# One core, DeltaNet and a cosine feed-forward: 66 places of a hand-written order and the queue of seven transfers are changed

## The chip, the cores and the metric

The kernel runs on one core of one Trainium2 chip. The metric is the device time of one execution in microseconds (us). PE is the matrix engine, PEld its weight loads, DVE the vector engine, ACT the scalar engine, POOL the third elementwise engine (GpSimd), and SP an engine that here only begins DMA transfers. SP and ACT each have a DMA queue (SPq, ACTq); the profile lists what an engine begins there beside its own work.

## The reference, cut to what matters

```python
def _attn_ref(q, k, v, beta):            # 4 batches, 8 heads, 768 steps, 48 wide
    k_n = k / (np.linalg.norm(k, axis=-1, keepdims=True) + 1e-06)
    state = np.zeros((B, H, D, D))
    for t in range(S):
        kt, vt, bt = k_n[:, :, t], v[:, :, t], beta[:, :, t, None]
        y[:, :, t] = np.einsum('bhd,bhde->bhe', q[:, :, t], state)
        v_old = np.einsum('bhde,bhd->bhe', state, kt)
        state = state + bt[:, :, :, None] * np.einsum('bhd,bhe->bhde', kt, vt - v_old)
    return y

def _moe_ref(x, w_in, w_out):            # 3072 tokens x 384, inner width 2048
    h = x @ w_in
    g = h * np.cos(h)
    return g @ w_out
```

The attention's output y, with heads side by side, is the x of the feed-forward part.

## The kernel before, in words

**Units and pairs.** The 768 steps are cut into 24 units of 32 steps. For each unit n, for all 32 pairs of batch and head, the kernel

- loads k, q and v (`load`, L383, issue L398; from unit 6 on k and q also in the layout of `load_blocks`, L411, issue L417),
- turns k and q over (`turn`, L637, `turn_out`, L648, ACT copy L652), takes the norms of k (`norms_square` L557 on ACT, `norms_sum` L562 on DVE, `norms_root` L574 on POOL, `scale`, L603 to L611, on DVE),
- forms the products of keys and queries with keys (`gram`, PE L675; `gram_keys` and `gram_queries` read them on DVE),
- needs the inverse of a triangular 32 x 32 matrix. For units 0 and 1 this is done by matrix products on PE, a chain of doublings: `double` (PE L759), `double_copy` (ACT L767), `double_turn` (DVE L772 and L775), `double_add` (DVE L779). In the task names, double (n, level, half). From unit 2 on it is done on POOL, for two units (a pair m) at once: `gram_put` (L833) writes the matrices to device memory, `gram_get` (L854) reads them back one matrix to a partition, `invert` (POOL L879 and L886, in pieces inv (m, i)) does the substitution, `put` (L891) writes the inverse and `get` (L902 for units 2 and 3, L910 later) brings it home for unit n. Units 2 and 3 are inverted in halves and have the steps solve_half (PE L960), half_out (ACT L972), between (PE L960) and between_out (DVE L980) more,
- multiplies the carried state with keys and queries (`state`, PE L930), solves for the update (`solve`, PE L996 for units 2 and 3, L1002 else; solve_out, DVE L1014), updates the state (`update`, PE L1027; update_out, DVE), multiplies within the unit (`within`, PE L1045 for the first units, L1057; within_out, ACT L1070) and gives the features of the feed-forward part (`features`, PE L1078; features_out, ACT L1086).

**The feed-forward part.** Two units make a pair p of 256 tokens. For pair 0 the inner product is plain: `hidden` (p, f) (PE L1099), then the cosine gate as `hidden_turns` (ACT L1136), `hidden_rest` (DVE L1143), `hidden_cos` (ACT L1152), `hidden_gate` (DVE L1155). Later pairs use fewer products on sums of blocks: `x_sum` (L1188, on POOL or DVE), `layer` (p, i) (PE L1273), layer_out (ACT L1285, L1287, or DVE L1290), then the gate, `product` (PE L1355; tasks named out), `collect` (L1407) and `store` (L1422).

**The weights** arrive in 28 pieces: `narrow_load` (issue L518; tasks named weights), `narrow_split` on ACT (L528, L532), `narrow_shift` on DVE (L536) and `narrow_add` on POOL (L540; tasks named split, shift, add). `keep_warm` (PE L495, tasks named warm) are matmuls whose result nobody reads.

**The order.** Every such step is a task with a key such as ('gram_put', 2). `Order.run` emits 2199 tasks in the order of `Order.LINE`, a list of the tasks' numbers. All instructions of one engine are pinned to that order, and all DMA issues of SP and ACT are also pinned to one common order. So the list fixes each engine's program, and an engine that waits for one task holds all that is behind it. A task that begins DMAs is issued by SP, or by ACT when its key stands in the set `Order.OTHER`; for `x_sum`, `left`, `right` and a few more the same set picks POOL or DVE:

```python
    def queue(*key):
        return nc.scalar if key in Order.OTHER else nc.sync

    def either(key, one, two):
        return two if key in Order.OTHER else one
```

An issue on ACT stands in ACT's program between its copies and activations.

Of the kernel before, what the change touches and what calls it, by code (L numbers as in the profile page):

```python
# [59 lines left out]
class Order:  # L60

    OTHER = {
        ('v', 0), ('v', 1), ('gram_put', 2), ('gram_put', 3), ('inv', 1, 0), ('put', 1),
        ('gram_put', 4), ('v', 5), ('gram_get', 2), ('put', 2), ('gram_put', 6), ('v', 8),
        ('v', 9), ('blocks', 9, 0), ('blocks', 9, 1), ('put', 4), ('get', 10), ('v', 11),
        ('blocks', 11, 0), ('blocks', 11, 1), ('gram_put', 11), ('gram_get', 5), ('v', 12),
        ('gram_put', 13), ('gram_get', 6), ('get', 13), ('v', 14), ('blocks', 14, 0), ('v', 15),
        ('blocks', 15, 0), ('blocks', 15, 1), ('v', 16), ('gram_put', 16), ('v', 17), ('k', 18),
        ('v', 18), ('get', 18), ('v', 20), ('gram_put', 21), ('gram_get', 11), ('store', 0, 1),
        ('right', 4, 4), ('left', 1, 1, 0), ('left', 1, 3, 0), ('left', 1, 3, 1),  # L70
# [23 lines left out]
        ('left', 10, 3, 1), ('store', 10, 1), ('x_sum', 11, 'd'), ('x_sum', 11, 'e'),  # L94
        ('x_sum', 11, 'k'), ('x_sum', 11, 'g'), ('x_sum', 11, 'f'), ('left', 11, 1, 0),
        ('left', 11, 2, 0), ('left', 11, 1, 1), ('left', 11, 3, 0), ('left', 11, 3, 1),
        ('store', 11, 1), ('store_right', 11), ('weights', 2), ('weights', 3), ('weights', 4),
        ('weights', 9), ('weights', 11), ('weights', 12), ('weights', 13), ('weights', 14),
        ('weights', 15), ('weights', 17), ('weights', 23), ('weights', 24)
    }  # L100

    WARM_FIRST, WARMS = 5, 17
    LINE = """
# [1845 lines left out]
```

## Time and profile before

| what | number |
|---|---|
| time, median of 3 runs | 640.1 us (638.85 to 642.2) |
| the profiled execution's own time | 642.77 us |
| its span in the trace | 641.0 us (1.77 us lie around it) |
| granted PE clock, mean | 0.98 |
| PE busy | 612.1 us (95%) |
| DVE busy | 504.4 us (79%) |
| POOL busy | 435.1 us (68%) |
| ACT busy | 297.5 us (46%) |
| DMA | 50.75 MB in 215844 packets, 207384 of them under 512 B |

The times of engines are shares of the span, so the share that PE leaves idle is an upper bound for what a new order of the same work can win, apart from the clock: the granted clock is the speed that PE was given, 1.00 being full. All times in the text are us from the span's start. "Idle before, with a releaser" is the time that an engine stood before an instruction, and what ended it by the profile.

### The profile page before, as it was taken

To read this page: it belongs to the slowest core of one execution; us is meant where nothing else is said; L and a number is where in the kernel's file an instruction comes from. 1 tells how busy PE (TensorE), PEld (TensorE's weight loads), DVE (VectorE), ACT (ScalarE), POOL (GpSimd) and SP (SyncE) were. 2 spreads that over 40 slices of the span, in tenths; PEclk is the share of its full clock that TensorE was granted. 3 is DMA by queue.
4 is the path that set the end of the run, shared out by engine and by line. 5 is a ranking of instruction groups with operands and counts; after the bars stand their busy time and mean duration, and the time that the engine had idled before them with its cause. 6 is when DMAs were issued, how large, how long until landed. Compare 5 with 4: busy or idle time off the path is not lost.

```text
span 641.0 us, 24058 instructions
## 1 busy us (share of the span) xinstructions
PE 612.1 (95%) x10096; PEld 571.4 (89%) x10096; DVE 504.4 (79%) x1051; ACT 297.5 (46%) x533; POOL 435.1 (68%) x791
## 2 busy tenths in 40 slices
PE   6978788999999999999999999999999999999997
PEld 4857777788799998999999999999999999999997
DVE  5876736999999897788878788978878676757872
ACT  3546535645543543543743553643544443635440
POOL 4428877788888888786886786888884881212231
PEclk8897979999999999999999999999999999999999
DMA  9876656655354645446234445333225011000001
GB/s 187 218 169 174 136 130 134 148 87 83 72 87 74 103 74 96 69 67 111 42 52 87 75 79 91 54 45 70 45 35 101 18 31 23 20 3 15 13 20 30
DMA packets 215844, 50.75 MB, mean 79 GB/s; under 512 B 207384, under 2 KB 210744, under 8 KB 215736
## 3 DMA queue, kind: packets, MB, share of 16 engines
q1 hardware_dynamic: 161132, 32.34, 27.8%
q10 hardware_dynamic: 54300, 16.33, 12.1%
q8 instruction: 79, 1.29, 0.8%
q0 software_dynamic: 304, 0.54, 0.4%
q14 instruction: 29, 0.24, 0.1%
HBM read 38.95 MB, written 10.22 MB: 77 GB/s over the span
## 4 chain that ended last, share of the span: by engine, by line
PE 76%; DMA 8%; POOL 5%; DVE 5%; issue 2%; SPq 2%; ACT 1%; ACTq 1%; DVEq 0%; POOLq 0%
PE p_out L1355 30%; PE p_h L1273 28%; PE p_kq L930 3%; PE p_s L1027 3%; POOL part L879 2%; POOL z L886 2%; PE p_u L1002 2%; PE p_kq L1057 2%; PE p_g L675 2%; PE p_h L1099 2%; DMA qp<-in_q_dram 2%; PE p_h L1355 2%; DMA kp<-in_k_dram 2%; PE p_z L1078 1%; DMA w_sum<-z_dr 1%
## 5 line engine op out<-in xcount | busy, mean ns | idle before, releaser
L879 POOL TENSOR_TENSOR part<-z,gb 128x126 f32<-128x126 f32 (+23 forms) x321 | 141.6, 441 | 44.1 <-DMA gb<-g_dr 17.5
L886 POOL TENSOR_TENSOR z<-z,part 128x126 f32<-128x126 f32 (+23 forms) x321 | 142.8, 445 | 25.2
L1355 PE MATMUL p_out<-w_out,g_ffn 128*128 128x192 f32 x672 | 121.0, 329 | 0.0
L1355 PEld LDWEIGHTS p_out<-w_out,g_ffn 128*128 128x128 f32 x672 | 107.9, 190 | 1.0
L1152 ACT ACTIVATE turns<-turns,halfpi 128x512 f32<-128x512 f32 x96 | 68.0, 718 | 83.2 <-DVE turns L1143 71.6
L1273 PE MATMUL p_h<-x_sum,w_in 128*128 128x128 f32 x704 | 92.3, 278 | 0.0
L1355 PE MATMUL p_out<-w_sum,g_ffn 128*128 128x192 f32 x496 | 88.7, 328 | 0.0
L1273 PEld LDWEIGHTS p_h<-x_sum,w_in 128*128 128x128 f32 x704 | 85.6, 191 | 1.9
L1136 ACT ACTIVATE turns<-g_ffn,quarter_turn 128x512 int32<-128x512 f32 x77 | 55.0, 719 | 66.3 <-DVE g_ffn L1155 35.4
L1355 PEld LDWEIGHTS p_out<-w_sum,g_ffn 128*128 128x128 f32 x496 | 79.6, 190 | 0.6
L1290 DVE TENSOR_TENSOR g_ffn<-g_ffn,p_h 128x512 f32<-128x512 f32 x88 | 59.5, 679 | 14.7 <-PE p_h L1273 13.7
L1155 DVE TENSOR_TENSOR g_ffn<-turns,g_ffn 128x512 f32<-128x512 f32 x77 | 61.7, 810 | 11.7 <-ACT turns L1152 11.6
L1143 DVE SCALAR_TENSOR_TENSOR turns<-g_ffn,turns 128x512 f32<-128x512 f32 x77 | 57.1, 750 | 8.2 <-ACT turns L1136 8.1
L1273 PE MATMUL p_h<-x_sum,in_sum 128*128 128x128 f32 x440 | 58.9, 278 | 0.8 <-POOL x_sum L1188 0.8
L1273 PEld LDWEIGHTS p_h<-x_sum,in_sum 128*128 128x128 f32 x440 | 54.3, 191 | 2.2 <-POOL x_sum L1188 1.0
L1070 ACT COPY y<-p_kq 32x384 f32<-32x384 f32 x96 | 45.1, 470 | 19.0 <-PE p_kq L1057 8.1
L1407 DVE SCALAR_TENSOR_TENSOR o<-p_out,o 128x192 f32<-128x192 f32 x74 | 25.1, 351 | 29.7 <-PE p_out L1355 29.5
L1273 PE MATMUL p_h<-x_ffn,w_in 128*128 128x128 f32 x352 | 46.6, 277 | 1.0 <-ACT p_h L1285 1.0
L1273 PEld LDWEIGHTS p_h<-x_ffn,w_in 128*128 128x128 f32 x352 | 43.0, 192 | 1.6 <-ACT p_h L1285 1.3
L574 POOL TENSOR_TENSOR knrm<-ksum,halves 128x16 f32<-128x16 f32 (+1 forms) x14 | 37.1, 2647 | 10.1 <-DVE ksum L562 9.5
L1371 POOL TENSOR_TENSOR g_ffn<-g_ffn 128x512 f32<-128x512 f32 x15 | 19.1, 1271 | 30.5 <-DVE g_ffn L1155 26.6
L1285 ACT COPY p_h<-p_h 128x512 f32<-128x512 f32 x44 | 25.3, 575 | 28.5 <-PE p_h L1273 20.4
(168 smaller groups left out, 1051.7 us busy)
## 6 DMA issues: line engine op xcount, KB each, us to landing
g_ffn<-in_moe_w_in_dram SPq DMA_DIRECT2D x7, 512.0 KB, 7.8
g_ffn<-in_moe_w_out_dram SPq DMA_DIRECT2D x9, 384.0 KB
kp<-in_k_dram SPq DMA_DIRECT2D x136, 24.0 KB, 2.5
gb<-g_dr SPq DMA_DIRECT2D x12, 256.0 KB, 3.9
g_ffn<-in_moe_w_out_dram ACTq DMA_DIRECT2D x7, 384.0 KB
g_ffn<-in_moe_w_in_dram ACTq DMA_DIRECT2D x5, 512.0 KB, 5.9
vp<-in_v_dram ACTq DMA_DIRECT2D x52, 48.0 KB, 2.7
zt<-z_dr SPq DMA_DIRECT2D x68, 32.0 KB, 2.7
```

The lines of the kernel that those rows point to most:

```text
L574: nc.gpsimd.tensor_tensor(out=scales[m][2][:, part], in0=sums[m, part.start][:, 0:n], in1=halves[:, 0:n], op=ALU.pow,)
L879: eng.tensor_tensor(out=part, in0=z[:, 0:rows, j, None].to_broadcast(shape), in1=a[:, j, None, j + 1 :].to_broadcast(shape), op=ALU.mult,)
L886: eng.tensor_tensor(out=behind, in0=behind, in1=part, op=ALU.subtract)
L1070: nc.scalar.copy(by_parity(y[quarter(b)]), p_kq[quarter(b ^ 1), :, b % 2])
L1136: nc.scalar.activation(turns[p, f], hidden_of(p, f), AF.Identity, bias=quarter_turn, scale=TURN)
L1143: nc.vector.scalar_tensor_tensor(out=r, in0=hidden_of(p, f), scalar=TURN, in1=t, op0=ALU.mult, op1=ALU.subtract,)
L1152: nc.scalar.activation(r, r, AF.Sin, bias=halfpi, scale=2.0 * math.pi)
L1155: nc.vector.tensor_tensor(out=place(p, f), in0=step_of(rests.pop((p, f)), f), in1=step_of(hidden_of(p, f), f), op=ALU.mult,)
L1273: nc.tensor.matmul(p_h[:, e], in_block(*w)[:, e], x_of(p, b), start=new and e == 0, stop=True, skip_group_check=True,)
L1285: nc.scalar.copy(to, part_of(p, one))
L1290: nc.vector.tensor_tensor(out=part_of(p, to), in0=part_of(p, one), in1=part_of(p, two), op=op)
L1355: nc.tensor.matmul(p_o, left(p, part, a)[:, e % 4], right(e, b), start=(e == 0), stop=(e == FT // 2 - 1), skip_group_check=True,)
```

## The change

No instruction is added or removed, apart from where DMAs are begun. In `Order.OTHER` five keys are struck: v 5, v 8, gram_put 4, gram_put 13 and weights 17 are now begun by SP instead of ACT. Two keys are new: weights 0 and gram_put 9 are begun by ACT instead of SP. In `Order.LINE` 66 numbers stand in another place. The moves up to some 60 us of the trace lie in the doubling chains of units 0 and 1, and around gram_put 2, which now comes ahead of the key loads of unit 5. Further moves, by engine (a task "now ahead of" others stood behind them before):

| engine | moves that the text speaks of |
|---|---|
| PE | double (1,3,0) now ahead of update 0; double (1,5,1) now behind features 0; state 2 ahead of hidden (0,2); hidden (0,6) ahead of between 2; state 3 ahead of warm 13; warm 14 behind between 3; gram 9 behind out (0,1,2); solve 6 ahead of layer (2,9); within 7 and gram 11 later; features 11 earlier |
| DVE | scale (3,0) behind solve_out 2, update_out 2 and several shifts; shift 20 ahead of shift 17; shift 26 later; update_out 7 earlier |
| POOL | add 18 ahead of add 17; norms 7 ahead of inv (5,0) |
| ACT | split 16 and split 26 later, split 18 earlier; half_out 3 ahead of cos (0,8); turns (0,12) earlier; eye 7 later |
| SP and ACT queues | gram_put 2 ahead of k 5; weights 17 behind get 2; weights 22 ahead of blocks (6,1) and get 3; gram_put 9 later; gram_put 15 and gram_get 7 behind put 6 and get 12 |

The diff, cut to its core (in the list, lines that differ only by shifted numbers are left out):

```diff
     OTHER = {
         ('v', 0), ('v', 1), ('gram_put', 2), ('gram_put', 3), ('inv', 1, 0), ('put', 1),
-        ('gram_put', 4), ('v', 5), ('gram_get', 2), ('put', 2), ('gram_put', 6), ('v', 8),
-        ('v', 9), ('blocks', 9, 0), ('blocks', 9, 1), ('put', 4), ('get', 10), ('v', 11),
+        ('gram_get', 2), ('put', 2), ('gram_put', 6), ('v', 9), ('blocks', 9, 0),
+        ('blocks', 9, 1), ('gram_put', 9), ('put', 4), ('get', 10), ('v', 11),
         ('blocks', 11, 0), ('blocks', 11, 1), ('gram_put', 11), ('gram_get', 5), ('v', 12),
-        ('gram_put', 13), ('gram_get', 6), ('get', 13), ('v', 14), ('blocks', 14, 0), ('v', 15),
+        ('gram_get', 6), ('get', 13), ('v', 14), ('blocks', 14, 0), ('v', 15),
...
-        ('store', 11, 1), ('store_right', 11), ('weights', 2), ('weights', 3), ('weights', 4),
-        ('weights', 9), ('weights', 11), ('weights', 12), ('weights', 13), ('weights', 14),
-        ('weights', 15), ('weights', 17), ('weights', 23), ('weights', 24)
+        ('store', 11, 1), ('store_right', 11), ('weights', 0), ('weights', 2), ('weights', 3),
+        ('weights', 4), ('weights', 9), ('weights', 11), ('weights', 12), ('weights', 13),
+        ('weights', 14), ('weights', 15), ('weights', 23), ('weights', 24)
     }
...
-1010 307 999 819 308 938 309 995 1011 812 996 397 351 352 939 353 1000 1002 311 1012 997 431 354 310
-282 341 804 399 283 940 379 1001 815 312 1004 432 380 1006 381 504 1013 933 1005 1014 313 314 382
+1010 307 999 819 308 938 309 995 1011 812 996 397 310 351 352 939 353 1000 1002 1012 997 431 354 282
+341 804 399 283 940 311 379 1001 815 312 1004 432 380 1006 381 504 1013 933 1005 1014 313 314 382
```

The last four lines show how a move looks: 310 is update_out 7, 311 is within 7.

52 rows, old and new, of the table LINE are left out of this document.

## The prediction

> **What bounds the kernel now.** First the table by windows, in two long stretches and around the drops of the clock. Its columns are the stretch, its length, the busy time of PE, of its weight loads, of DVE, ACT and POOL (instructions in brackets), the granted clock, the DMA engines' share and GB/s.
>
> ```profile
> span 641.0 us, 24058 instructions
> 0.00:118.00 118.00, 94.86 (x2193) 83.45 (x2196) 81.05 (x212) 59.97 (x119) 76.33 (x131) 0.90 0.70 161
> 118.00:641.00 523.00, 517.28 (x7916) 487.92 (x7912) 423.34 (x840) 237.56 (x414) 358.74 (x661) 1.00 0.35 61
> 38.63:42.05 3.42, 2.01 (x36) 1.38 (x34) 2.91 (x9) 0.00 (x0) 0.09 (x1) 1.00 0.99 215
> 52.29:55.70 3.41, 2.00 (x89) 1.69 (x85) 2.77 (x14) 3.36 (x7) 2.75 (x4) 1.00 0.88 262
> 55.70:62.53 6.83, 6.83 (x105) 6.19 (x102) 5.25 (x16) 4.16 (x9) 5.58 (x17) 0.50 0.66 176
> 83.01:89.84 6.83, 6.21 (x138) 5.90 (x134) 2.15 (x7) 2.58 (x5) 5.58 (x17) 0.50 0.89 254
> ```
>
> PE bounds the end. After 118 us it idles 523.00 − 517.28 = 5.7 us, the tail included, and its work there isn't changed by the edits. Before 118 it idles 118.00 − 94.86 = 23.1 us, and the clock takes more: in 83.01 to 89.84 PE was busy 6.21 us at 0.50, so that it did 3.1 us' worth. So a reorder can win about 23 us of waiting plus some half-clock stretches, all early; anything later can only be lost or pass through.
>
> Next I read PE's timeline in the double-chain stretch (start, busy, line, and in brackets the idle time before it and its releaser), and ACT's beside it.
>
> ```profile
> 45.91 0.68 PE L759 MATMUL p_h<-in_sum 64*64 64x64 f32 x16 [1.02 <-ACT in_sum L767]
> 49.42 0.89 PE L1027 MATMUL p_s<-u,kp 64*64 64x96 f32 x32 [0.74 <-DVE u L1014]
> 51.42 1.13 PE L759 MATMUL p_h<-w_sum 64*64 64x64 f32 x32
> 53.62 1.15 PE L930 MATMUL p_kq<-st,kq_t 48*64 48x48 f32 x64 [1.07 <-ACT y L1070]
> 55.11 0.68 PE L759 MATMUL p_h<-w_sum 64*64 64x64 f32 x16 [0.34 <-DVE w_sum L772]
> ...
> 43.27 2.17 ACTq L833 DMA_DIRECT2D g_dr<-g  x2
> 45.48 0.37 ACT L767 COPY in_sum<-p_h 128x256 f32<-128x256 f32 x1 [7.37 <-DVE w_in L536]
> ```
>
> Four gaps are named here. ACT stood 7.37 us: at the head of its queue was gram_put 2 (L833), and the copy for the next double waited behind it.
>
> **The change part by part.** (1) *36 to 58 us.* gram_put 2 goes ahead of the unit-5 key loads. The page names DVE as releaser of the 7.37 us, but the two ACT issues end at 45.44 (43.27 + 2.17), just ahead of the copy, so the queue held it. Transfers wait for each other in this kernel: counted over both hardware queues in program order, an issue in the trace begins when the one eight places before it has landed. An example:
>
> ```profile
> 77.14 5.76 SPq L417 DMA_DIRECT2D qp<-in_k_dram  x4
> ```
>
> Four issues take 5.76 us, where four of get 6 in (4) take 1.81: the group ends at 82.90 (77.14 + 5.76), just after a piece of get 2 landed at 82.57 (75.95 + 6.62, the chain in (2)). So a put moved ahead of loads waits for older landings and starts earlier. What lies behind it, gram_put 3, still waits for key pieces. That caps the gain at the 1.02 us that PE waits at 45.91; below, the bound is 0, since solve 0 also needs unit 4's keys. I take 0.2. Double (1,3,0) moves in front of update 0: its half of the 1.13 us (16 of 32 matmuls, 0.56) falls into the 0.74 gap. Double (1,5,1), the other half, leaves its place before state 1 for one after features 0. State 1 waits for ACT y either way, so the gap of 1.07 grows by 1.13 to 2.2, less what arrives early, and the 0.56 comes back as work later, part of it into the 0.34 gap. Sum at 58.7 us: −0.2 − 0 + (0.56 − 0.34) = about 0. The clock window 52.29 to 55.70 idled 1.41 us and was followed by half clock; 38.63 to 42.05 idled as much and wasn't. The wider gap makes this drop no less likely, and it is there already.
>
> (2) *The second unit's block data, 74 to 92 us.*
>
> ```profile
> 79.18 0.24 PE L960 MATMUL p_w<-rhs,w_sum 32*32 32x48 f32 x2 [0.61 <-DMA w_sum<-z_dr]
> 84.87 1.50 PE L960 MATMUL p_v<-g_ffn,in_sum 32*32 32x48 f32 x64 [0.62 <-ACT g_ffn L972]
> 86.30 4.62 PE L1099 MATMUL p_h<-x_ffn,w_in 128*128 128x128 f32 x24
> 91.66 2.94 PE L1099 MATMUL p_h<-x_ffn,w_in 128*128 128x128 f32 x24
> ...
> PE p_w L960 <- DMA w_sum<-z_dr: 3.7, 3, 2.2
> ...
> 75.95 6.62 DMA w_sum<-z_dr
> ...
> 75.90 0.54 ACTq L518 DMA_DIRECT2D g_ffn<-in_moe_w_out_dram  x1
> ```
>
> The waits say that solve_half 2 stood 3.7 us in three waits for get 2's pieces; the chain of waits shows the last one 6.62 us in flight, to 82.57. Weights 17 (384 KB) was begun on ACT at 75.90 beside it. At the 254 GB/s of the window after, 384 KB are 1.5 us of the engines. The change begins weights 17 on SP behind get 2: the gain lies between 0 (the small pieces are slow by themselves) and 1.5. I take 0.85, the middle. Weights 17 then lands late, but its split stands behind half_out 2 and is covered by the hidden group that follows. Hidden (0,6) goes in front of between 2: it fills the 0.62 us gap and opens one of the like size before solve 2, which then waits for DVE; 0. The gram_put 4 move spares SP a wait, but PE's next reader doesn't wait for it. So −0.85 here; of it I keep half, −0.4, to 118 us, between 0 and −0.85, because waits that others end stay: ACT work on half_out 3, DVE's solve outputs. State 3, half_out 3, v 5 on SP and warm 14 move around short gaps; warm 14 now stands behind between 3, and I put them at 0 together.
>
> (3) *POOL.* Scale (3,0) moves out of DVE's idle time to behind update_out 2, and add 18 ahead of add 17.
>
> ```profile
> 87.56 0.17 DVE L603 TENSOR_TENSOR knrm<-knrm,tiny 128x16 f32<-128x16 f32 x1
> ...
> 88.59 0.19 DVE L611 TENSOR_TENSOR bz<-bs,consts 128x32 f32<-128x32 f32 x1
> ...
> 95.53 1.02 POOL L540 TENSOR_TENSOR w_out<-w_out,g_ffn 128x384 uint32<-128x384 uint32 x1
> 97.98 2.97 POOL L540 TENSOR_TENSOR w_out<-w_out,g_ffn 128x384 uint32<-128x384 uint32 x3 [1.44 <-issue]
> 100.90 0.43 POOL L879 TENSOR_TENSOR part<-z,gb 128x135 f32<-128x135 f32 x1
> 126.66 1.02 POOL L540 TENSOR_TENSOR w_out<-w_out,g_ffn 128x384 uint32<-128x384 uint32 x1 [2.29 <-ACT turns L1152]
> ```
>
> The first and last of scale's five instructions span 1.22 us (88.59 + 0.19 − 87.56), which now lie in DVE's busy time. POOL did add 17 at 95.53 in idle time; now it stands until shift 18 is done and then does all four adds, so that inverse 2 goes on at 100.90 + 1.0 (one add) + 0.7 (later shift) = 102.6. The 2.29 us gap at 126.66 takes the 1.8 us. Cost 0; without that cover, 1.8 on POOL.
>
> (4) *Solve 6.* It goes ahead of layer (2,9); v 8 goes from ACT to SP behind get 6.
>
> ```profile
> 175.16 1.16 PE L1273 MATMUL p_h<-x_sum,in_sum 128*128 128x128 f32 x8 [0.75 <-POOL x_sum L1188]
> 177.04 1.06 PE L1273 MATMUL p_h<-x_sum,in_sum 128*128 128x128 f32 x8
> 178.68 0.67 PE L1002 MATMUL p_u<-rhs,zt 64*64 64x48 f32 x30 [0.34 <-DMA zt<-z_dr]
> ...
> 173.60 1.81 SPq L910 DMA_DIRECT2D zt<-z_dr  x4
> ...
> 175.30 3.09 ACTq L398 DMA_DIRECT2D vp<-in_v_dram  x4
> ```
>
> Get 6's last piece ended this wait of 0.34. Layer (2,9), 1.06 us, was PE's work until then. If get 6 lands as before, PE waits 1.06 us more, and the layer comes after. With v 8 out of its way the last piece can land earlier, by 0 to 1.1 us: v 8 began at 175.30, between get 6's issues. Inverse 3 starts up to 0.6 later, by the shift of split 26 and add 26 on POOL. So this costs between 0 and 1.7; I take 0.7, near the layer's whole price, less some of v 8's.
>
> (5) *Inverse 7.* gram_put 15 and gram_get 7 move behind put 6 and get 12.
>
> ```profile
> 291.58 1.68 SPq L833 DMA_DIRECT2D g_dr<-g  x3
> 295.63 1.13 SPq L854 DMA_DIRECT2D gb<-g_dr  x2
> 297.31 1.81 SPq L910 DMA_DIRECT2D zt<-z_dr  x4
> ...
> 304.08 0.69 POOL L879 TENSOR_TENSOR part<-z,gb 128x31 f32<-128x31 f32 x1
> ...
> 344.70 1.81 SPq L910 DMA_DIRECT2D zt<-z_dr  x4
> ...
> 350.87 0.68 PE L1002 MATMUL p_u<-rhs,zt 64*64 64x48 f32 x32
> ```
>
> gram_get 7 came 4.05 us after gram_put 15; started at 299.12, the put lets it go at 303.2, 7.5 us later. From gram_get's 295.63 to inverse 7's 304.08 are 8.45 us; the page's row of issues gives such a get 3.9 us to landing, so the start slips by 303.2 + 3.9 − 304.08 = 3.0 us. At the other end get 14 was issued by 346.51 and solve 14 ran at 350.87; with some 2 us for landing about 2 us of slack are left, and put 7's wait is shorter if inverse 7 meets fewer adds. I take 0; the bound is +1.
>
> The other moves after 118 us (gram 9 and 11, update_out 7, within 7, norms 7, features 11, gram_put 13) pass work that PE does anyway, at 0.
>
> **Sum.** −0.4 (2) + 0.7 (4) = +0.3 us: 642.8 becomes 643.1 for an execution such as the profiled one (642.77 us, 1.77 around its span), which lies 0.4% over the median of 640.1 shown. In that median's terms: 640.4 us. Bounds without the clock: −1.02 (1) − 0.85 (2) = −1.9, and +1.7 (4) + 1.0 (5) = +2.7.
>
> **Rivals.** *A, faster: a half-clock stretch falls away.* With get 2 earlier and state 1's surroundings changed, one of the stretches at 55.70 and 83.01 doesn't come: 3.1 to 3.4 us of work at full speed (half of 6.21 and of 6.83), with the −0.4 about 3.6. For it: 52.29 to 55.70 idled 1.41 us, the edge that another window passed. Against it: the move widens the gap just there. And a lead of PE must reach POOL's inverse 3, else it is waited away at solve 6. 640.1 − 3.6 = 636.5 us.
>
> *B, slower: the wait for get 6 throws the clock.* It decides where v 8's move doesn't help: a wait of 0.34 + 1.06, with the slip of inverse 3 up to 2.0 us, exceeds 1.41 us in one clock window, and 6.83 us of a full PE run at half speed: 1.1 + 3.4 − 0.4 = +4.1, or 644.2 us. For it: no work stands between. Against it: the page shows 1.41 once harmless.
>
> The Trainium skill, "TensorE: Matmul & The Clock Gate", section "What's actually happening", has the clock fall after an idle window of about 3.4 us, and by that rule a 2 us wait costs only itself: B would come to 640.8. The trace differs, as the half clock at 55.70 follows 1.41 us of idle in two pieces.
>
> *C: inverse 7 reaches solve 14 late* by the whole 3 us: 643.4, if the slack read above isn't there.
>
> *D: nothing comes of it.* PE is full after 118 us and each gap is only passed on: 640.1, which lies in the forecast's own range.
>
> **How the numbers follow.** Forecast with D, 638.2 to 642.8 (the bounds −1.9 and +2.7): 0.47. A: 0.29. B: 0.15. C: 0.09, about half of it over the bound. The range must take in A and B: 635.8 to 644.8. Changes under 0.5% (3.2 us) are about what a measurement of this kernel can't tell from none. Faster by over that: A, less what is waited away, plus the get 2 gain in full, 0.29. Slower: B and half of C with the tails, 0.21. Same: 0.50.
>
> **What would show it.** (1) ACT's 7.37 us gap falls to below 6 and state 1's gap rises to about 2; (2) the 3.7 us of get 2 waits fall to under 3; (3) inverse 2 goes on at 102 to 103, and no PE row names it; (4) the wait for zt before solve 6 is 1 to 1.4 us; (5) inverse 7 starts near 307. Half clock in the windows after 175 would show B, a clock above 0.90 before 118 A. The prediction fails if the chain of POOL moves by more than 2 us either way, since the late waits of PE all hang on it.

## The result, and the profile after

The changed kernel takes 647.2 us (median of 4 runs, 646.2 to 650.6) against 640.3 us before: 1.0115 of the time before, 95% interval 1.0068 to 1.0163. It is slower by some 7 us, above the forecast of 640.4 and above the upper end of the range, 644.8. The profiled execution took 647.97 us, its span 646.2 us.

The stages of the trace after, in the columns of the table by windows quoted for before:

```profile
span 646.2 us, 24065 instructions
0.00:118.00 118.00, 96.87 (x2231) 83.10 (x2232) 86.94 (x222) 63.55 (x125) 79.63 (x133) 0.96 0.73 170
118.00:647.00 529.00, 515.11 (x7867) 487.04 (x7866) 416.53 (x831) 235.19 (x409) 359.82 (x659) 0.99 0.33 58
```

The early stage looks better: PE is busier, and the clock is 0.96 instead of 0.90. PE's timeline gives the place at which the feed-forward output of pair 0 begins (L1297, task out (0,0,0)): 112.44 us, where the trace before had 118.33. So PE was 5.9 us ahead, and lost that and 5.2 us more behind it: 11.1 us. Of these, PE's busy time behind that place, 516.96 us before and 520.67 after, has 3.7 us, and its idle time, 5.71 before and 13.09 after, 7.4 us. PE's waits and POOL's show where, first the one line of before that counts here, then those of after:

```profile
PE p_u L1002 <- DMA zt<-z_dr: 0.3, 1, 0.3
```

```profile
PE p_u L1002 <- DMA zt<-z_dr: 2.8, 4, 1.0
PE p_out L1355 <- DVE o L1407: 2.4, 2, 2.2
PE p_h L1273 <- DVE g_ffn L1290: 2.2, 1, 2.2
...
POOL part L879 <- ACT z L867: 10.1, 2, 7.6
```

PE's lines have us in total, times and the longest: the waits for inverses (zt) grew from 0.3 to 2.8 us, and two waits of 2.2 us for DVE are new. Of the 2.8 us, 1.70 lie at solve 10 and 1.13 at solve 22 (538 to 539 us); the latter no run here isolates. The last line is POOL's: it stood 7.6 us at the start of an inverse for ACT L867, the step eye. Norms, scale, eye and inverse are numbered by pair of units, solve and get by unit: inverse 5 serves solves 10 and 11, and norms 8 the units 16 and 17. The rows lie behind 200 us, in this order (start, busy, line, idle before and its releaser):

```profile
213.41 2.90 POOL L574 TENSOR_TENSOR knrm<-ksum,halves 128x16 f32<-128x16 f32 x1 [1.62 <-DVE ksum L562]
216.27 0.24 POOL L879 TENSOR_TENSOR part<-z,gb 128x31 f32<-128x31 f32 x1
...
257.82 0.28 PE L1002 MATMUL p_u<-rhs,zt 64*64 64x48 f32 x2 [0.98 <-DMA zt<-z_dr]
258.82 0.68 PE L1002 MATMUL p_u<-rhs,zt 64*64 64x48 f32 x30 [0.72 <-DMA zt<-z_dr]
...
299.81 4.54 ACTq L910 DMA_DIRECT2D zt<-z_dr  x4
304.40 0.72 ACT L1136 ACTIVATE turns<-g_ffn,quarter_turn 128x512 int32<-128x512 f32 x1 [5.41 <-DMA zt<-z_dr]
307.12 0.60 ACT L867 COPY z<-consts 128x512 f32<-128x512 f32 x1
...
307.17 1.57 PE L1355 MATMUL p_out<-w_out,g_ffn 128*128 128x192 f32 x8 [2.17 <-DVE o L1407]
...
307.80 0.24 POOL L879 TENSOR_TENSOR part<-z,gb 128x31 f32<-128x31 f32 x1 [7.56 <-ACT z L867]
334.20 2.91 POOL L574 TENSOR_TENSOR knrm<-ksum,halves 128x16 f32<-128x16 f32 x1
...
337.14 0.32 DVE L603 TENSOR_TENSOR knrm<-knrm,tiny 128x16 f32<-128x16 f32 x1 [4.63 <-POOL knrm L574]
338.85 0.67 DVE L1290 TENSOR_TENSOR g_ffn<-g_ffn,p_h 128x512 f32<-128x512 f32 x1
...
339.58 2.08 PE L1273 MATMUL p_h<-x_ffn,w_in 128*128 128x128 f32 x8 [2.17 <-DVE g_ffn L1290]
...
339.40:346.20 6.80, 6.62 (x136) 6.01 (x140) 5.41 (x13) 2.01 (x3) 6.10 (x13) 0.50 0.47 75
```

The rows of before at the same steps, norms 7, eye 7, get 13, norms 8 and scale 8:

```profile
220.83 2.90 POOL L574 TENSOR_TENSOR knrm<-ksum,halves 128x16 f32<-128x16 f32 x1
302.82 0.60 ACT L867 COPY z<-consts 128x512 f32<-128x512 f32 x1
304.03 1.82 ACTq L910 DMA_DIRECT2D zt<-z_dr  x4
331.28 2.91 POOL L574 TENSOR_TENSOR knrm<-ksum,halves 128x16 f32<-128x16 f32 x1
334.41 0.17 DVE L603 TENSOR_TENSOR knrm<-knrm,tiny 128x16 f32<-128x16 f32 x1
```

Two chains are to be seen. **At 213 us** POOL waits 1.62 us for the sum of norms 7 and works 2.90 us on it, with inverse 5 queued behind; solve 10 then waits 0.98 + 0.72 us for that inverse. The 2.90 us are no added work, since before they stood inside inverse 5; what is added on POOL is the wait. **At 300 us** ACT begins get 13 and stands in it: four issues take 4.54 us, where the same four took 1.82 before. DVE stands 2.83 us for the turns (ACT L1136) that come behind get 13, so that a collect (L1407) further on in DVE's program is late, and PE waits 2.17. ACT reaches eye 7 at 307.12, so that inverse 7 begins at 307.80, not 304.08, although PE was ahead. Norms 8 stands on POOL in the middle of inverse 7, at 334.20 instead of 331.28. DVE stands 4.63 us at the step scale 8, which needs those norms; the layer additions (L1290) stand behind it, and PE waits for them, 2.17 us. The clock then falls to 0.50 for 6.8 us with a full PE: some 3.3 us more.

### The profile page after: what moved, and what is told of

Read it like the earlier page. It is cut to its first block, busy times and chain, and to the rows that moved or that the text cites. A ratio compares the mean times of both kernels' runs of the same rounds, so it can differ in the third digit from the quotient of the medians.

```text
span 646.2 us, 24065 instructions
## 1 busy us (share of the span) xinstructions
PE 612.0 (95%) x10096; PEld 570.1 (88%) x10096; DVE 503.5 (78%) x1051; ACT 298.7 (46%) x533; POOL 439.4 (68%) x791
## 3 DMA queue, kind: packets, MB, share of 16 engines
q8 instruction: 79, 1.29, 0.8%
## 4 chain that ended last, share of the span: by engine, by line
PE 44%; POOL 31%; DMA 10%; issue 6%; SPq 3%; DVE 3%; ACT 1%; ACTq 1%; POOLq 0%; DVEq 0%
PE p_out L1355 18%; PE p_h L1273 16%; POOL z L886 13%; POOL part L879 13%; DMA gb<-g_dr 2%; SPq L398 2%; DMA kp<-in_k_dram 2%; DMA z_dr<-z 2%; PE p_h L1355 2%; PE p_kq L930 2%; DMA zt<-z_dr 2%; POOL w_out L540 2%; PE p_g L675 1%; POOL knrm L574 1%; PE p_h L759 1%
## 5 line engine op out<-in xcount | busy, mean ns | idle before, releaser
L886 POOL TENSOR_TENSOR z<-z,part 128x126 f32<-128x126 f32 (+23 forms) x321 | 147.5, 460 | 25.1
L1136 ACT ACTIVATE turns<-g_ffn,quarter_turn 128x512 int32<-128x512 f32 x77 | 55.0, 720 | 74.8 <-DVE g_ffn L1155 31.5
L1290 DVE TENSOR_TENSOR g_ffn<-g_ffn,p_h 128x512 f32<-128x512 f32 x88 | 59.4, 678 | 12.8 <-PE p_h L1273 11.9
L1407 DVE SCALAR_TENSOR_TENSOR o<-p_out,o 128x192 f32<-128x192 f32 x74 | 25.1, 352 | 29.8 <-PE p_out L1355 29.7
```

Source lines behind the costliest of these rows:

```text
L886: eng.tensor_tensor(out=behind, in0=behind, in1=part, op=ALU.subtract)
L1136: nc.scalar.activation(turns[p, f], hidden_of(p, f), AF.Identity, bias=quarter_turn, scale=TURN)
L1290: nc.vector.tensor_tensor(out=part_of(p, to), in0=part_of(p, one), in1=part_of(p, two), op=op)
```

## The experiments

A word on the numbers. One kernel's executions lie here up to some 7 us from their median, so the ratio with its interval decides, and a trace tells places and reasons. A trace can be far from its kernel's median: e4's execution took 640.5 us (median 647.1), e12's 648.8 (median 645.1). To compare traces, the span is cut at the start of out (0,0,0). The part behind that cut doesn't hold the accidents of the early clock, but it has accidents of its own: in the seven traces whose order up to there is that of the change (after, e1, e3, e4, e5, e9, e10), PE's wait for DVE near 191 us is between 0.28 and 2.07 us. The table has each kernel's ratio to the kernel before (95% interval), the cut, and the span minus the cut.

| kernel | ratio | cut, us | span − cut, us |
|---|---|---|---|
| before | 1 | 118.33 | 641.0 − 118.33 = 522.7 |
| before again (e7) | | 112.30 | 522.9 |
| 30 fillers (e11) | 1.0053 (1.0012 to 1.0095) | 117.81 | 521.2 |
| early moves only (e8) | 0.9998 (0.9970 to 1.0026) | 115.23 | 523.4 |
| solve 6 group alone (e14) | 0.9988 (0.9955 to 1.0021) | 115.67 | 525.0 |
| unit 7 group alone (e13) | 1.0031 (0.9997 to 1.0066) | 112.62 | 525.6 |
| norms 7 alone (e6) | 1.0037 (1.0010 to 1.0065) | 116.67 | 525.6 |
| two transfers alone (e15) | 1.0039 (1.0011 to 1.0067) | 116.41 | 526.5 |
| eye 7 alone (e12) | 1.0066 (1.0029 to 1.0104) | 120.19 | 526.9 |
| after, groups a and b back (e1) | 1.0024 (0.9995 to 1.0053) | 112.81 | 526.5 |
| after, b back (e4) | 1.0107 (1.0035 to 1.0178) | 111.85 | 526.9 |
| after, a back (e3) | 1.0062 (1.0025 to 1.0100) | 115.66 | 528.1 |
| groups a and b alone (e2) | 1.0133 (1.0064 to 1.0202) | 113.19 | 531.2 |
| after, get 13 on SP (e5) | 1.0088 (1.0059 to 1.0118) | 112.77 | 531.2 |
| after, eye 7 back (e9) | 1.0108 (1.0042 to 1.0173) | 113.14 | 531.7 |
| after, norms 8 first (e10) | 1.0182 (1.0118 to 1.0245) | 117.89 | 531.7 |
| after | 1.0115 (1.0068 to 1.0163) | 112.44 | 533.8 |

Group a is gram_put 15 (number 513 of the list), gram_get 7 (514), eye 7 (515) and the cosine 1246; group b is inv (5,0), number 406, behind norms 7. The diffs show the moved numbers with their neighbours in the list.

**Groups a and b back, and alone.**

```diff
 # e1, from the changed kernel
-1172 441 513 514 1234
+466 467 513 1240 1165
+1167 1226 514 1168 1295
-1246 1254 515 1296 1174
+1234 563 515 1173 1253
-395 1105 406 1033 1044
+1082 483 406 331 484
 # e2, from the kernel before: the same the other way round
```

> The changed kernel with two late groups put back to their old places: gram_put 15, gram_get 7, eye 7 and one cosine (group a), and norms 7 against inv (5,0) (group b). Theory L (the loss is made by these two groups, the early moves gain): PE keeps the 6.0 us by which the changed kernel was ahead at 118 us, less about 1.5 us given back at solves that wait for POOL, so 4 to 6 us under the kernel before: 634 to 636 us. Rival P (the lead of PE can't be kept, because POOL's inverses bound every later solve, whatever the late order): 639 to 641 us, with new waits for zt at the solves from 6 on.

> The kernel before with groups a and b alone moved as in the change. Theory L: inverse 7 starts 3 to 4 us late and PE, which isn't ahead here, waits some 2 to 4 us between 300 and 350 us, with a half-clock stretch (3.3 us) possible: 643 to 648 us. Rival P: the late moves cost nothing without the lead, since inverse 7 had slack: 639 to 641 us.

e2 took 1.0133 of the time before (649.6 us, above the 643 to 648 of theory L), as much as the whole change: the two groups make the loss, as theory L has it. Its trace has both waits of PE, 2.07 us at 308.40 and 1.75 at 340.44, and no half clock behind them, so the half clock at 339.4 of the trace after isn't what the loss needs. In e1, though, the forecast gain didn't come: 1.0024, so 0 to 3 us slower, not 4 to 6 faster. The trace of e1 is 5.5 us ahead at the cut and keeps 1.7 us of it. That half of theory L fell. And e2, whose early order is that of the kernel before, was 5.1 us ahead at the cut too (113.19). The lead wasn't the early moves' work.

**One group back at a time.**

```diff
 # e3, from the changed kernel: 513, 514, 515 and 1246 as in e1
 # e4, from the changed kernel: 406 as in e1
```

> The changed kernel with group a alone put back; norms 7 stays ahead of inv (5,0). Theory L, group a being the larger: the 7.6 us of POOL's idle time before inverse 7 and both 2.2 us waits of PE between 300 and 340 us go, with the half clock at 340: 636 to 639 us. Rival P: 640 to 643 us.

> The changed kernel with group b alone put back: inverse 5 starts some 4 us earlier than in the changed kernel, the waits of PE for zt at solve 10 (1.7 us in all) go. Theory L: what comes after, the late inverse 7, still stops PE between 300 and 345 us: 644 to 647 us, 0 to 2 us under the changed kernel. Rival N (norms 7 is the larger cause, since it delays inverse 5 and with it inverses 6 and 7): 637 to 641 us.

Without a, 1.0062; without b, 1.0107: by the medians a is the larger, as expected, but the two intervals overlap. Both lie above 1. e4's trace still has POOL's idle time before inverse 7 (6.28 us) and PE's wait near 335 (1.75 us); e3's has neither, and waits 1.18 + 0.67 us for zt at solve 10 instead. Both fit the two chains read above. e3's time, 645.5 us, is over what either theory said, and e4's, 647.1, is at the upper end of theory L's; rival N fell.

**The kernel before once more, and the early moves alone.**

```diff
 # e8, from the kernel before: only moves that lie before 160 us, and
-('gram_put', 4), ('v', 5), ('weights', 17),
+('weights', 0),
```

> The kernel before, unchanged, for a second trace. If the half-clock stretches before 118 us come by the chance of where the clock's windows fall, this trace has other stretches than the first (11.3 to 21.6, 55.7 to 62.5, 83.0 to 89.8) and PE reaches pair 1's first product up to 6 us earlier or later than at 118.3. If they belong to the order, the same three stretches show, and 118.3 within 1 us.

> The kernel before with only those moves and queue changes of the change that lie before 160 us. Theory K (the early moves do gain waits, and give-backs come from the later moves): 2 to 4 us under the kernel before, 637 to 639 us. Rival P (the early moves gain nothing that lasts, since PE's lead is waited away at the solves): 640 to 641 us, ratio within 0.5% of 1.

e7 is the same program as before. Its windows (the columns as above), and the start of out (0,0,0) in PE's timeline:

```profile
span 635.2 us, 24058 instructions
0.00:118.00 118.00, 95.98 (x2232) 82.65 (x2233) 89.45 (x220) 62.30 (x124) 82.36 (x137) 0.96 0.75 168
72.80:76.20 3.40, 0.97 (x10) 0.67 (x8) 3.40 (x8) 1.93 (x4) 3.25 (x4) 1.00 1.05 222
76.20:83.00 6.80, 4.86 (x131) 4.43 (x132) 2.68 (x7) 2.59 (x5) 5.47 (x18) 0.52 0.69 197
...
112.30 0.91 PE L1297 MATMUL p_out<-w_out,g_ffn 128*128 128x384 f32 x2
```

The unchanged program reaches out (0,0,0), the place that the expectation calls pair 1's first product, at 112.30 us, 6.0 us sooner than in the first trace, and its span is 635.2 instead of 641.0. Nothing of its order differs; the clock does: it is 0.96 over the early stage, as in the trace after, and not 0.90. The stretches at 55.7 and 83.0 are not there, another one lies at 76.2 to 83.0, after a window with 2.4 us of idle time. So the 5.9 us lead of the changed kernel is no gain of the change: e7 against after is 112.30 against 112.44. e8 says the same by times: the early moves alone take 0.9998 of the time before, with 0.3% to either side. Theory K fell, and rival P is right about the result.

**Group a, piece by piece.**

```diff
 # e5, from the changed kernel (OTHER): get 13 begun by SP
-('get', 13),
 # e9, from the changed kernel
-1246 1254 515 1296 1174
+1234 563 515 1173 1253
 # e12, from the kernel before
-1234 563 515 1173 1253
+1246 1254 515 1296 1174
 # e15, from the kernel before
-466 467 513 1240 1165
-1167 1226 514 1168 1295
+441 513 514 1234 563
```

> The changed kernel, get 13 alone begun by SP instead of ACT. In the changed kernel ACT stood 5.4 us at get 13, whose third and fourth issue are the eighth transfers behind gram_get 7. Theory Q (the loss of group a is this stand of ACT, from which eye 7, the cosine and PE's wait of 2.2 us at 307 follow): ACT's gap at 304 falls below 2 us, inverse 7 starts near 304, held by gram_get 7's landing alone, PE's waits at 307 and 340 go: 641 to 643 us, near the kernel with group a put back (645.5, interval 1.0025 to 1.0100). Rival D (gram_put 15 and gram_get 7 are simply late, wherever get 13 is begun): inverse 7 still starts at 307 to 308, PE still waits, and the time stays at 646 to 648 us.

> The changed kernel with eye 7 and one cosine alone put back on ACT, ahead of get 13; gram_put 15 and gram_get 7 stay late. Theory E (inverse 7 started at 307.8 because eye 7 stood on ACT behind get 13 and two cosines): inverse 7 starts when gram_get 7 lands, 3 to 3.5 us earlier, norms 8 in its middle too, and PE's wait of 2.2 us near 340 falls below 0.5; the wait near 307, which ACT's stand at get 13 makes, stays: 642 to 645 us. Rival D (the transfers' own lateness is all): 646 to 648 us as the changed kernel.

> The kernel before with eye 7 and one cosine alone moved as in the change; its transfers stay. Theory E: eye 7 ends some 3 us later on ACT, inverse 7 starts at its end, about 3 us late, norms 8 too, and PE waits up to 1 us near 340: 641 to 643 us. Rival D: without the late transfers ACT doesn't stand at get 13, eye 7 is late by only the two cosines, and nothing is lost: 640 to 641 us.

> The kernel before with gram_put 15 and gram_get 7 alone moved behind put 6 and get 12; eye 7 stays ahead of get 13. Theory Q: ACT stands at get 13 until gram_get 7 has landed, 2 to 4 us, PE waits up to 2 us near 308, inverse 7 starts some 2.5 to 3.5 us late (its data): 642 to 645 us. Rival E only: with eye 7 in place the lateness of the transfers is hidden in POOL's additions ahead of inverse 7: 640 to 641.5 us.

First e12's rows at inverse 7 and at the late wait, then e15's at get 13, inverse 7 and the early wait:

```profile
310.03 0.60 ACT L867 COPY z<-consts 128x512 f32<-128x512 f32 x1
...
310.71 0.24 POOL L879 TENSOR_TENSOR part<-z,gb 128x31 f32<-128x31 f32 x1 [5.18 <-ACT z L867]
...
342.62 1.16 PE L1273 MATMUL p_h<-x_ffn,w_in 128*128 128x128 f32 x8 [1.76 <-DVE g_ffn L1290]
```

```profile
301.25 3.23 ACTq L910 DMA_DIRECT2D zt<-z_dr  x4
304.53 0.72 ACT L1136 ACTIVATE turns<-g_ffn,quarter_turn 128x512 int32<-128x512 f32 x1 [3.88 <-DMA qp<-in_q_dram]
...
304.31 0.24 POOL L879 TENSOR_TENSOR part<-z,gb 128x31 f32<-128x31 f32 x1 [2.96 <-DMA gb<-g_dr]
...
307.48 1.57 PE L1355 MATMUL p_out<-w_out,g_ffn 128*128 128x192 f32 x8 [1.03 <-DVE o L1407]
```

Eye 7 alone costs 0.66% (4.2 us): it ends at 310.6 (310.03 + 0.60), POOL stands 5.18 us for it, and the late wait of PE is there, with no early one. The transfers alone cost 0.39% (2.5 us): ACT stands at get 13 (3.23 us for the four issues), POOL stands 2.96 us for the data, and PE waits 1.03 us near 307, with no wait near 340. So theory E has one chain, theory Q the other, and the rival fell in both. Theory E had the size wrong: it gave 641 to 643 us, a start 3 us late and a wait of up to 1 us, and 645.1, 5.18 and 1.76 came. Half clock follows e12's wait too: 342.4 to 349.2 ran at 0.75 on average. In e5, with get 13 on SP, the early wait of PE is gone from the trace, as theory Q has it, but inverse 7 still starts at 309.05, since eye 7 stands behind its cosine:

```profile
308.37 0.60 ACT L868 COPY z<-consts 128x512 f32<-128x512 f32 x1
...
309.05 0.24 POOL L880 TENSOR_TENSOR part<-z,gb 128x31 f32<-128x31 f32 x1 [4.63 <-DMA zt<-z_dr]
...
341.08 1.16 PE L1274 MATMUL p_h<-x_ffn,w_in 128*128 128x128 f32 x8 [1.68 <-DVE g_ffn L1291]
```

(In e5, e9, e10 and e14 the lines stand one further down, in e11 two.) The profile names a DMA as releaser of the 4.63 us, but get 13's issues, of which the third and fourth wait for gram_get 7 to land, had ended at 308.08 on SP, so the data was there; eye 7 ended last, at 308.97 (308.37 + 0.60). e5's time, 645.5 us, lies between theory Q's 641 to 643 and rival D's 646 to 648, and its interval overlaps that of after. Theory Q alone doesn't settle group a. In e9, eye 7 is early, and POOL's idle time before inverse 7 is 1.93 us, with gb as its releaser; no wait near 340 is left, and the one near 307, which theory E kept, is down to 0.28 us. The time stays at 1.0108 (647.2 us) all the same, inside rival D's range and not theory E's. These rows of its trace lie at solve 10:

```profile
262.15 0.28 PE L1003 MATMUL p_u<-rhs,zt 64*64 64x48 f32 x2 [1.85 <-DMA zt<-z_dr]
263.13 0.95 PE L1003 MATMUL p_u<-rhs,zt 64*64 64x48 f32 x30 [0.69 <-DMA zt<-z_dr]
```

The wait at solve 10, by norms 7, is 1.85 + 0.69 us, where after had 1.70, and half clock follows; near 191 and 209 us PE waits 2.07 and 1.28 us, where after had 0.63 and 0.25. That is one execution; that it makes up for eye 7 in the median isn't shown. With intervals of 0.5 to 0.7% to either side, e9 and after can still differ by the 0.66% of e12. So eye 7's cost is shown where it alone is moved (e12), and not where it alone is put back (e9).

**Norms 7 alone, and norms 8 first.**

```diff
 # e6, from the kernel before
-1082 483 406 331 484
+395 1105 406 1033 1044
 # e10, from the changed kernel: norms 8 is 539, inv (7,5) is 521
-1180 520 521 1306 1249
-1278 1279 539 540 597
+538 539 521 1317 1315
```

> The kernel before with norms 7 alone moved ahead of inv (5,0). Theory: norms 7 waits there for its sum on DVE, and inverse 5 starts later by that wait and its 2.9 us, some 4 us in all less POOL's gap of 0.8; solve 10 then waits for get 10 by 1.5 to 2 us: 642 to 643 us. Rival: the step is hidden, as POOL has 1.9 us of idle time before inverse 6: 639 to 641 us.

> The changed kernel with norms 8 ahead of inv (7,5) on POOL, some 3.7 us earlier. Theory M (the wait of PE near 340 is norms 8, queued on POOL in the middle of the late inverse 7, then scale 8 on DVE, which holds the additions that PE's layers wait for): DVE's idle time of 4.6 us before scale 8 and PE's wait of 2.2 us with the half clock behind it go: 642 to 645 us. Rival G (it is inverse 7's end, put 7 and get 14 that stop PE): solve 14 waits 1 to 3 us instead, and the time stays at 646 to 648 us.

e6's rows on POOL and at solve 10:

```profile
217.44 2.90 POOL L574 TENSOR_TENSOR knrm<-ksum,halves 128x16 f32<-128x16 f32 x1 [1.63 <-DMA vp<-in_v_dram]
220.31 0.24 POOL L879 TENSOR_TENSOR part<-z,gb 128x31 f32<-128x31 f32 x1
...
262.38 0.28 PE L1002 MATMUL p_u<-rhs,zt 64*64 64x48 f32 x2 [0.70 <-DMA zt<-z_dr]
263.24 0.68 PE L1002 MATMUL p_u<-rhs,zt 64*64 64x48 f32 x30 [0.58 <-DMA zt<-z_dr]
```

Norms 7 costs 0.37% (2.4 us; 643.1 us, at the upper end of the theory's range). PE waits 1.28 us at solve 10 in the trace; the idle time of 1.9 us before inverse 6 didn't hide it, so the rival fell. In e10, DVE's idle time before scale 8 fell from 4.63 to 0.41 us, and no wait of PE is left near 340: theory M's place is confirmed.

```profile
339.90 0.37 DVE L604 TENSOR_TENSOR knrm<-knrm,tiny 128x16 f32<-128x16 f32 x1 [0.41 <-POOL knrm L575]
...
356.45 0.28 PE L1003 MATMUL p_u<-rhs,zt 64*64 64x48 f32 x2 [0.52 <-DVE o L1408]
357.08 0.68 PE L1003 MATMUL p_u<-rhs,zt 64*64 64x48 f32 x30 [0.35 <-DMA zt<-z_dr]
376.38 0.78 PE L1003 MATMUL p_u<-rhs,zt 64*64 64x48 f32 x32 [1.33 <-ACT x_ffn L1087]
```

But the time didn't fall: 1.0182 (652.3 us), above what either side expected. Norms 8's 2.9 us now come before two pieces of inverse 7, and solves 14 and 15 wait 0.52, 0.35 and 1.33 us. The lateness can be moved from one wait to another. Part of the 652 us isn't explained by this: span − cut is 2.1 us less than after, the cut itself 5.4 us later.

**The other late moves.**

```diff
 # e13, from the kernel before: update_out 7, within 7, gram 11, its keys
-431 354 310 282 341
-1000 1002 311 1012 997
-820 355 400 356 357
+996 397 310 351 352
+283 940 311 379 1001
+1071 1072 400 401 403
 # e14, from the kernel before: layer (2,9) behind solve 6, gram 9 later; OTHER
-977 985 982 276 813
-895 958 345 959 893
+966 927 982 316 816
+903 801 345 346 348
-('v', 8)
+('gram_put', 9)
```

> The kernel before with update_out 7, within 7, gram 11, its keys and one sum of pair 3 moved as in the change, nothing else. Theory U (these make the waits of PE for DVE near 191 and 209 us, 1.2 to 3.4 us in all in the kernels that have them): one or both waits show, 1 us or more together, and gram_put 11 comes later on ACT: 641.5 to 643 us. Rival: the waits belong to another late move: under 0.5 us there, 640 to 641 us.

> The kernel before with the moves around solve 6 alone: solve 6 ahead of layer (2,9), v 8 on SP, gram 9 later and gram_put 9 on ACT. As predicted: PE waits 0.3 to 1.7 us for get 6 before solve 6, and the time is 640.5 to 642 us. Rival: v 8's move lets get 6 land early enough that PE doesn't wait at solve 6 at all, as in the changed kernel's trace: 640 to 640.8 us.

e14 shows solve 6, whole, without a wait: the rival held, and no cost of the group is measured (0.9955 to 1.0021).

```profile
174.66 0.68 PE L1003 MATMUL p_u<-rhs,zt 64*64 64x48 f32 x32
```

e13's ratio leaves 0 to 0.7% open. Its trace has a wait of 0.61 us at 210.81 and none at 191, where e1, with the same moves, waits 1.55 and 1.29 us. And e14's trace, which has none of these moves, waits at both places, 0.61 us at 192.83 and 0.71 at 214.35. So the waits belong not to these moves alone, and theory U is not shown; the moves around solve 6 play a part in them, whose cost stays open.

**Filling PE's early gaps.**

```diff
 # e11, from the kernel before (and 30 places in the list, as the expectation says)
-    WARM_FIRST, WARMS = 5, 17
+    WARM_FIRST, WARMS = 5, 47
```

> The kernel before with 30 more matmuls that nobody reads (0.43 us each), put where its PE idles before 118 us: 3 before gram 0, 7 before double (0,0,0), 1 to 2 before double (0,3,1), double (0,4,1), update 0, state 1, update 1, gram 5, between 2, between 3 and update 3, and 6 before solve_half 2. No order is changed. Theory C (the early stage is set by half-clock stretches, which follow clock windows with 1.4 us or more of idle time): the stretches between 10 and 118 us, 10 to 24 us long in the traces so far, fall below 7 us, and the time falls by 3 to 6 us: 634 to 638 us. Rival W (PE's lead is waited away later, or the added matmuls hold PE where they run over): 640 to 642 us.

```profile
0.00:118.00 118.00, 103.75 (x2273) 87.57 (x2274) 83.18 (x214) 60.40 (x119) 78.81 (x133) 0.99 0.73 165
...
117.81 1.56 PE L1299 MATMUL p_out<-w_out,g_ffn 128*128 128x384 f32 x4
```

The clock rose to 0.99, as wanted, but out (0,0,0) begins at 117.81, and the time is 1.0053 (1.0012 to 1.0095) of that before. PE was busy for 7.8 us more than in e7 (103.75 − 95.98), and the filling held the work up by more than the clock gave. Theory C is right about the clock and wrong about the time; rival W is right, and by its second reason: behind the cut e11 loses nothing (521.2 us, the least in the table). No kernel here beats the one before.

## Why the prediction was wrong

*What bounds the kernel* held: PE is full after 118 us, and what is late there is lost. The trace after shows PE waits of 0.2 to 2.2 us there and one half-clock stretch that before didn't have.

*(1), (2), the early moves.* Their places were read rightly. State 1's gap rose to 2.01 us (forecast about 2), ACT's gap of 7.37 us fell to 1.78, and the waits for get 2's pieces, 3.7 us before, are no longer among those that the profile lists; a part of that fall may be chance, since e7, the unchanged order, has 2.4. (The middle of 0 and 1.5 is 0.75, not 0.85; the sum hardly changes.) The sum, −0.4, lies inside e8's interval, 0.9970 to 1.0026. What wasn't seen is that the profiled execution before was an unlucky one: its clock over the whole span, 0.977, is the lowest of the 84 executions of that kernel that the experiments are compared with (the others have 0.978 to 0.995). With the clock either full or half, 0.90 over the early stage is (1 − 0.90) × 2 × 118 = some 24 us at half clock, and e7, the same order, at 0.96 has some 9. The prediction took the three stretches as the kernel's own and priced rival A by them.

*(3), inverse 2* was covered: POOL waited 1.37 us and did four additions at 93.42, and inverse 2 went on at 97.30; no wait of PE follows from it. The sign "102 to 103" didn't come, as all of the early stage was sooner; measured from out (0,0,0), inverse 2 went on 2.3 us later than before (17.4 us ahead of it before, 15.1 after), and 1.7 was forecast.

*(4), solve 6*, the largest term at +0.7, was 0: get 6's last piece landed before the solve, and the sign of 1 to 1.4 us didn't come. Rival B named the right mechanism at a wrong place. A wait with half clock behind it came in the trace after, at 339.58, not at 178.

*(5), inverse 7, is the step that failed.* "The start slips by 3.0 us" is right for the transfers: where they alone are moved (e15), POOL stands 2.96 us. That inverse 7 then began at 307.80 in the changed kernel, near the forecast 307, is luck. There gram_get 7 had landed by 304.35, when get 13's issues, which wait for it, had ended; eye 7, in no term of the prediction, ended at 307.72 and set the start; and all of this came with PE ahead. Measured from out (0,0,0), inverse 7 began 195.4 us behind it after and 185.8 before: 9.6 us later, far over the 2 us at which the prediction said that it would fail. "I take 0; the bound is +1" was wrong, twice. The slack was read at inverse 7's end, get 14 against solve 14; but on POOL norms 8 stands in the middle of inverse 7, so all that DVE does behind scale 8 is late from 334 on, before get 14 matters. And ACT was left out. Get 13 is begun by ACT, and by the rule of eight places that (1) uses it now stands behind gram_get 7; eye 7, moved by the same change, is behind get 13. In place of 0, eye 7 alone costs 0.66% (4.2 us) and the two transfers alone 0.39% (2.5 us).

*"The other moves … pass work that PE does anyway, at 0"* failed for norms 7: it was moved on POOL, not past PE's work, and it waits there for its sum: 0.37%. These three make 1.4% (0.66 + 0.39 + 0.37); e2, which has them together, measured 1.33%, the whole change 1.15%. Each has an interval of 0.3 to 0.7% to either side, so the sum fits, but the shares are rough.

*Rival C* had the direction and the place, inverse 7, and 3.0 us; what came is two to three times that, as eye 7, ACT's stand and norms 7 add up. Its mechanism, a late solve 14, didn't come: between 339.58 and 451.44 the trace after has no wait of PE.

## What to carry to other kernels

When a start slips, look for who else is queued in the middle of the slipped work on its engine, and not only for the reader of its end: here norms 8, inside an inverse of 35 us, made PE wait, and the inverse's own end didn't. A transfer moved later also moves the ones that are counted behind it, on both queues, and the one that is begun by a computing engine holds that engine up. And take a second trace of the same kernel before pricing anything by its clock: here two of them differ by 6.0 us at the same instruction.

## What the runs showed of the hardware

The granted clock fell to half after single waits of about 2 us. In the trace after, 336.0 to 339.4 had 1.99 us of idle time, and 339.4 to 346.2 ran at 0.50. The like wait at 307.17 (2.17 us), in a window of 3.4 us with PE idle for 2.2, was followed by full clock. So with the waits at solve 10: 1.70 us in the trace after, with full clock behind them, and 1.73 us in e5's (1.09 + 0.64), where 261.8 to 268.6 ran at 0.75 on average. The rows of the trace after:

```profile
336.00:339.40 3.40, 1.41 (x39) 1.13 (x26) 2.12 (x7) 0.00 (x0) 3.01 (x7) 1.00 0.00 0
304.00:307.40 3.40, 1.23 (x81) 0.98 (x70) 2.25 (x6) 2.25 (x4) 0.00 (x0) 1.00 0.35 47
307.40:310.80 3.40, 3.40 (x25) 3.40 (x25) 2.96 (x5) 3.28 (x7) 2.46 (x8) 1.00 0.30 55
```

The Trainium skill, "TensorE: Matmul & The Clock Gate", section "What's actually happening", speaks of an idle window of about 3.4 us; the drop at 339.4 came after less, and the measurement decides. A free-running window, which that section also has, would let one wait of 2.2 us lie in one window and another be cut by an edge; where the edges lay at 307 no run here shows, so this reason is not shown.
